# Late attention groups: reading all scores of a group first, sharing one weight buffer between three chunks, and turning the weights as a step of its own

## The chip, the core and the metric

The kernel runs on one NeuronCore of one Trainium2 chip. The metric is the device time of one execution in microseconds (us). A core has a matrix engine (PE, TensorE), whose weight loads are listed apart as PEld, a vector engine (DVE), a scalar engine (ACT), a general engine (POOL, GpSimd) and a sync engine (SP) that issues most DMA transfers. Every engine works off its own queue in order: an instruction that waits holds up all that stand behind it on the same engine.

## What is computed

Block-causal attention over 8 batches, 8 heads, 576 positions and head size 64, and a gated two-layer network on its output, all in float32:

```python
scores = q @ k.T / sqrt(64)                    # per batch and head
scores = where(block(i) >= block(j), scores, -1e9)   # blocks of 64 positions
attn = softmax(scores) @ v
x = attn, heads side by side                   # 4608 tokens x 512
h = x @ w_in                                   # 512 -> 2048
out = (h * sigmoid(1.702 * h)) @ w_out         # 2048 -> 512
```

## The kernel before

**Network.** The 4608 tokens are cut into 12 tiles of 384. For each of 16 slices `fc` of the hidden layer, `moe()` multiplies the tile with `w_in` (12 matmuls into a PSUM bank `hp`), ACT takes the tanh (line 621), DVE forms the gate (622), ACT rounds it to `gh` (633) and POOL takes the rest `gl` (through the helper `subtract`, line 83). The second product of a slice (9 matmuls into the banks `acc`) is issued only after the first product of the *next* slice, so that the gate has the time of one first product. Each product is made of three matmuls of high and low parts. At the end of a tile `split(t + 1)` cuts the next tile into `xh` (ACT, 557) and `xl` (DVE, 83).

**Attention.** Work goes by groups of one batch and two heads, 32 in all. The 576 query rows are five chunks (0 to 4) that see 64, 192, 320, 448 and 576 keys. `score` multiplies q and k into PSUM banks, chunks 3 and 0 side by side in one bank for each head, and 2 and 1 in another. `weigh` reads a score on DVE with the mask and a running extremum (line 378) into an SBUF tile `e`, and ACT takes the exponential in place, with its sum (385). `normalise` forms the reciprocal of the sum (DVE 395, 400) and scales `e`: on POOL (405), and for chunk 4 of a late group on DVE (407).

**Early and late groups.** Groups 0 to 7 are early: PE transposes their weights (`flip`). From group 8 on they are late: `turn` transposes 32 by 32 blocks on DVE (414, 419) into `turned`, and after chunk 4 it has SP issue 16 DMAs (426) that put these blocks in their places. `av` multiplies them with v. All late groups use the same two halves of `turned`: the turns of a group must wait for the 16 DMAs of the group before, which read what the turns write. A late group takes chunks 3, 0, 2 and 1 in `score`, and chunk 4 in `av` of the group before, in the step's item `V`. In `settle`, the loop of one bank pair is: read its chunks, then normalise and turn them, then go on to the next pair. The weight tile of chunk `i` is

```python
e = d2.tile([P, 2, w], F32, tag=f"e{i % 2}", name="e", bufs=1)
```

so that chunks 0, 2 and 4 take turns in one buffer, and chunks 3 and 1 in another: chunk 1 can't be read before chunk 3 is turned, nor chunk 2 before chunk 0 is.

**Score banks.** In the late stage `bank()` goes round three PSUM banks, `w0` to `w2`; a fourth is lent by the network, which otherwise alternates between two banks for `hp`. The outputs of `av` take banks from the same round, so `av` waits until the scores in them are read.

**The order of the work.** The PE order is written out by hand. `ORDER` gives each step (one group) a line of slots, 13 in a late step: an item, or `-` for nothing. After each slot `advance` issues network work up to a quota that grows evenly, and goes on to the next gate. `START` and `HANDOVER` are the lines of steps 4 and 8. On the other engines, the framework orders instructions by when they can start in its own estimate and by priority, not strictly as written; tanh, gate, `gh`, `gl` and `split` have a higher priority (`high_priority`). PE's matmuls and chunk 4's first `normalise` instruction keep the written order. One further order is forced: the third gate after a group's `score` is put behind the last score read on DVE (`behind`, 108 and 625 to 627).

Of the kernel before, what the change touches and what calls it, by code (L numbers as in the profile page):

```python
# [10 lines left out]
F32 = mybir.dt.float32  # L11
# [14 lines left out]
ORDER = (  # L26
# [3 lines left out]
)  # L30

START = "1+0 - B 2/3 L C - V - 4 - a - - -"
HANDOVER = "B C - 3+0/2+1 - - - - - - V - - - - -"


WEIGHTS_BY = ((0, 0), (8, 13), (14.5, 32))
# [4 lines left out]
def attention_moe_kernel(  # L41
# [9 lines left out]
    nc = tc.nc  # L51
    B, H, S, D = q.shape
    DM, DF = w_in.shape
    P = 128
    BLK = 64
# [7 lines left out]
    NPAIR = B * H // 2  # L63
    HP = H // 2
# [4 lines left out]
    d2 = ctx.enter_context(tc.tile_pool(name="d2", bufs=2))  # L69
# [5 lines left out]
    def early(n):  # L75

        return n < 2 * HP

    def phase(n):
        return 0 if n < HP else 1 if n < 2 * HP else 2  # L80
# [3 lines left out]

    turns = {"n": 0, "bank": 0, "experts": False, "late": False, "gates": 0}
    gate_bank = {"now": "h", "spare": "w3", "lent": False}
    conv = {"step": 0, "loaded": 0}

# [11 lines left out]
    def next_hp():  # L102
# [1 line left out]
            gate_bank["now"], gate_bank["spare"] = gate_bank["spare"], gate_bank["now"]  # L104
        gate_bank["lent"] = False
        return ps.tile([P, 512], F32, tag=gate_bank["now"], name="hp")

    def behind(ins, other):
        tc.add_manual_dep(
            ins.ins, other.ins.name, mybir.DependencyInfo(mybir.DependencyClass.NoSync, mybir.DependencyReason.DATA),  # L110
            reason="order on one engine",
        )

    def mm(**kw):
        return tc.keep_in_program_order(nc.tensor.matmul(**kw))  # L115
# [60 lines left out]
    es = []  # L176
# [4 lines left out]
    def width(i):  # L181
        return BLK * (2 * i + 1)
# [125 lines left out]
    def prep(n):  # L308

        tag = "e0" if early(n) and n % 2 else "qk"  # L310
        qk[n] = d2.tile([P, 2, S], F32, tag=tag, name="qk", bufs=1)
        for x in range(2):
            nc.vector.transpose(out=qk[n][:, x], in_=raw[n][:, x].rearrange("p c d -> p (c d)"))  # L313
        raw.pop(n)
        m = follower(n)
        if m is not None:
            load(m)
# [3 lines left out]
    def score(n, banks):  # L321

        turns["late"] = not early(n)
        turns["gates"] = 0
        if n not in stats:
            mx = d2.tile([P, NCH + 1, 2], F32, tag="mx", name="mx")
            sm = d2.tile([P, NCH, 2], F32, tag="sm", name="sm")
            stats[n] = (mx, sm)
        todo = []
        taken = 0  # L330
        for chunks in banks:

            part = []
            for lo, hi in ((0, 512),) if width(chunks[0]) <= 512 else ((0, 256), (256, S)):
                ss = []
                for _ in range(2):
                    taken += 1
                    ss.append(lent_bank() if taken == 1 and turns["late"] else bank())
                c = 0
                for i in chunks:  # L340
                    a, z = qrange(i)
                    w = min(hi, width(i)) - lo
                    for hd in range(2):
                        r = slice(hd * D, hd * D + D)

                        mm(
                            out=ss[hd][:, c : c + w], lhsT=qk[n][r, 0, a : a + P],
                            rhs=qk[n][r, 1, lo : lo + w], start=True, stop=True,
                        )
                        part.append((i, hd, lo, lo + w, ss[hd][0 : z - a, c : c + w]))  # L350
                    c += w
            todo.append(sorted(part, key=lambda x: (chunks[::-1].index(x[0]), x[2])))
        settle(n, banks, todo)

    def settle(n, banks, todo):
        for chunks, part in zip(banks, todo):
            e = {}
            for i, hd, lo, hi, s in part:
                e[i] = weigh(n, i, hd, lo, hi, s, e.get(i))
            if not early(n) and 4 in chunks and n + 1 < NPAIR:  # L360
                prep(n + 1)
            for i in chunks[::-1]:
                normalise(n, i, e[i])
                if not early(n):
                    turn(n, i, e[i])

    def weigh(n, i, hd, lo, hi, s, e):
        mx, sm = stats[n]
        a, z = qrange(i)
        m = z - a  # L370
        w = width(i)
        if early(n):
            e = es[i]
        elif e is None:
            e = d2.tile([P, 2, w], F32, tag=f"e{i % 2}", name="e", bufs=1)
        last = i > 0 and hi == w
        mk = mask[0:m, MW - (hi - lo) : MW] if last else mask[0:m, 0 : hi - lo]
        turns["read"] = nc.vector.tensor_tensor_reduce(  # L378
            out=e[0:m, hd, lo:hi], in0=s, in1=mk,
            op0=ALU.add, op1=ALU.min, scale=-0.125,  # L380
            scalar=3e38 if lo == 0 else mx[0:m, NCH, hd : hd + 1],
            accum_out=mx[0:m, i, hd : hd + 1] if hi == w else mx[0:m, NCH, hd : hd + 1],
        )
        if hi == w:
            nc.scalar.activation(  # L385
                out=e[0:m, hd], in_=e[0:m, hd], func=AF.Exp, scale=-1.0,
                bias=mx[0:m, i, hd : hd + 1], accum_out=sm[0:m, i, hd : hd + 1],
            )
        return e

    def normalise(n, i, e):
        _, sm = stats[n]
# [125 lines left out]
        return None if m is None or m >= NPAIR else m  # L518

    def order(n):  # L520
        return {HP: START, 2 * HP: HANDOVER}.get(n, ORDER[phase(n)]).split()

    def step(n):

        turns["n"] = n
        now = n < NPAIR

        def item(x):
            if x == "V":
                return (lambda: av(n - 1)) if n else None  # L530
            if x == "L":
                return (lambda: prep(n + 1)) if n + 1 < NPAIR else None
            if x in ("a", "B", "C"):
                m, chunks = {"a": (n, [0, 1]), "B": (n - 1, [2, 3]), "C": (n - 1, [4])}[x]
                return (lambda: flip(m, chunks)) if m >= 0 else None
            return (lambda: score(n, [[int(z) for z in y.split("+")] for y in x.split("/")])) if now and x != "-" else None

        return [item(x) for x in order(n)]
# [29 lines left out]
    def moe():  # L568
# [24 lines left out]
        for t in range(NT):  # L593
            tt = TILES[t][1]
            if t == 0:
                yield ("tile", 0)
                split(0)
            xh, xl = xs["xh"], xs["xl"]
            acc = [ps.tile([P, DM], F32, tag=f"acc{c}", name=f"acc{c}") for c in range(tt // P)]
            for fc in range(NFC):  # L600
                if t == 0:
                    convert(fc // FG * GROUP + NDC + fc % FG + 1)
                hp = next_hp()
                fs = slice(fc % FG * P, (fc % FG + 1) * P)
                terms = [(wa, xb, dc) for dc in range(NDC) for wa, xb in (("wih", xh), ("wil", xh), ("wih", xl))]
                if fc == 0:

                    terms.sort(key=lambda x: x[1] is xl)
                for cnt, (wa, xb, dc) in enumerate(terms):
                    mm(  # L610
                        out=hp[:, 0:tt], lhsT=weights(wa, fc // FG)[:, dc, fs], rhs=xb[:, dc, 0:tt],
                        start=cnt == 0, stop=cnt == 3 * NDC - 1,
                    )
                    if cnt % 3 == 2:
                        yield unit1(tt)
                g = d2.tile([P, TT], F32, tag="g", name="g", bufs=1)[:, 0:tt]
                gh = d2.tile([P, TT], F32R, tag="gh", name="gh")[:, 0:tt]
                gl = d2.tile([P, TT], F32R, tag="gl", name="gl")[:, 0:tt]

                with tc.high_priority(offset=300):  # L620
                    nc.scalar.activation(out=g, in_=hp[:, 0:tt], func=AF.Tanh, scale=1.702)  # L621
                    gate = nc.vector.scalar_tensor_tensor(  # L622
                        out=g, in0=g, scalar=1.0, in1=hp[:, 0:tt], op0=ALU.add, op1=ALU.mult
                    )
                    turns["gates"] += 1
                    if turns["late"] and turns["gates"] == 3:
                        behind(gate, turns["read"])

                if fc == NFC - 1 and t + 1 < NT:
                    yield ("tile", t + 1)  # L630
                    split(t + 1)
                with tc.high_priority(offset=300):
                    nc.scalar.copy(out=gh, in_=g)  # L633
                    subtract(nc.gpsimd, gl, g, f(gh))
                yield ("gate", fc)
                if prev is not None:
                    yield from second(prev)
                prev = (gh, gl, fc, acc, t)
# [88 lines left out]
```

## Time and profile before

| what | value |
| --- | --- |
| median of 3 runs | 1112.54 us (1110.59 to 1112.55) |
| the profiled execution | 1109.89 us |
| its span, first to last instruction | 1108.1 us |
| PE busy | 1065.1 us (96% of the span) |
| DVE, ACT, POOL busy | 585.0, 497.8, 405.1 us |
| late scores, first to last read on DVE | 187.0 to 938.8 us |

The profiled execution took 1.8 us more than its span and 2.65 us less than the median of the runs. In the profile, L378 is line 378 of the kernel; a releaser behind an arrow is what ended the idle time of an engine. Matmuls are pipelined and their ends are modelled, so PE's idle time is a lower bound of what PE loses. The program's tile names in the profile are `e` for the weights, `bank` for scores and attention outputs, `mx` and `sm` for extrema and sums, `g`, `gh`, `gl` for the gate and its parts. The turned weights and the DMAs between them are `turned`.

### The profile page before, as it was taken

The numbers are of one execution on the slowest core, as the hardware profiler recorded it, in microseconds if no ns is written. First come the engines' busy times: TensorE is split into PE (matmuls) and PEld (weight loads), VectorE is DVE, ScalarE is ACT, GpSimd is POOL, SyncE is SP. The second block draws the span as 40 slices with busy tenths as digits, with TensorE's granted clock in tenths as the row PEclk, the third lists the DMA queues.
The fourth block names the chain that finished last, engine by engine and source line by source line (L and its number), as shares of the span: only waits on it lengthen the run. The fifth ranks groups of instructions, "written<-read, shape, count | busy, mean of one in ns | idle before, by whom it ended". The sixth has DMA issues, their size and how long they took to land. (4 is left out here: it accounts for less than half of the span.)

```text
span 1108.1 us, 19988 instructions
## 1 busy us (share of the span) xinstructions
PE 1065.1 (96%) x6960; PEld 913.5 (82%) x6960; DVE 585.0 (53%) x1856; ACT 497.8 (45%) x1321; POOL 405.1 (37%) x509
## 2 busy tenths in 40 slices
PE   5969999989999999999999999999999999999998
PEld 3757777878888888788888888788888888999997
DVE  6786786555655655554555555455546655211211
ACT  6866776433533534444443543344444434332322
POOL 5665665323333233233333332333333333222222
PEclk9979999999999999999999999999999999999999
DMA  8634623432333443143444433244443322200000
GB/s 182 198 90 155 153 55 80 87 90 60 92 80 81 114 87 82 37 108 74 104 87 86 93 88 70 48 104 86 87 114 70 73 81 55 55 29 1 29 1 29
DMA packets 219365, 91.25 MB, mean 82 GB/s; under 512 B 197760, under 2 KB 197760, under 8 KB 219264
## 3 DMA queue, kind: packets, MB, share of 16 engines
q1 hardware_dynamic: 214528, 89.38, 34.2%
q8 instruction: 55, 0.90, 0.3%
q10 hardware_dynamic: 4736, 0.59, 0.3%
q14 instruction: 46, 0.38, 0.1%
HBM read 45.09 MB, written 9.44 MB: 49 GB/s over the span
## 5 line engine op out<-in xcount | busy, mean ns | idle before, releaser
L83 POOL TENSOR_TENSOR gl<-g,gh 128x384 fp32r<-128x384 f32 x192 | 194.1, 1011 | 501.0 <-ACT gh L633 345.4
L622 DVE SCALAR_TENSOR_TENSOR g<-g,hp 128x384 f32<-128x384 f32 x192 | 104.6, 545 | 323.7 <-ACT g L621 323.5
L115 PE MATMUL hp<-xh,wih 128*128 128x384 f32 x768 | 261.2, 340 | 4.0 <-DVE g L622 2.8
L621 ACT ACTIVATE g<-hp 128x384 f32<-128x384 f32 x192 | 94.4, 492 | 374.4 <-PE hp L115 319.7
L115 PE MATMUL hp<-xh,wil 128*128 128x384 f32 x768 | 258.5, 337 | 0.0
L115 PE MATMUL hp<-xl,wih 128*128 128x384 f32 x768 | 255.2, 339 | 0.7 <-DVE xl L83 0.5
L115 PE MATMUL acc<-woh,gh 128*128 128x512 f32 x576 | 233.0, 405 | 3.5 <-ACT gh L633 3.5
L115 PE MATMUL acc<-wol,gh 128*128 128x512 f32 x576 | 227.8, 396 | 0.0
L115 PE MATMUL acc<-woh,gl 128*128 128x512 f32 x576 | 168.1, 393 | 0.3 <-POOL gl L83 0.3
L405 POOL TENSOR_TENSOR e<-e,sm 64x64 f32<-64x64 f32 (+1 forms) x192 | 114.5, 612 | 135.3 <-ACT e L385 83.2
L115 PEld LDWEIGHTS hp<-xh,wih 128*128 128x128 f32 x768 | 144.4, 188 | 18.4 <-DVE g L622 4.6
L633 ACT CAST gh<-g 128x384 fp32r<-128x384 f32 x192 | 98.5, 513 | 124.5 <-DVE g L622 124.4
L115 PEld LDWEIGHTS hp<-xh,wil 128*128 128x128 f32 x768 | 144.4, 188 | 7.6
L115 PEld LDWEIGHTS hp<-xl,wih 128*128 128x128 f32 x768 | 143.9, 188 | 2.4 <-DVE xl L83 2.4
L385 ACT ACTIVATE e<-e,mx 64x64 f32<-64x64 f32 (+4 forms) x240 | 132.4, 555 | 26.0 <-DVE mx L378 26.0
L115 PEld LDWEIGHTS acc<-woh,gh 128*128 128x128 f32 x576 | 108.7, 189 | 32.1 <-ACT gh L633 8.3
L115 PE MATMUL bank<-qk 64*128 64x192 f32 (+5 forms) x768 | 120.0, 424 | 14.4 <-DVE qk L313 11.5
L115 PEld LDWEIGHTS acc<-woh,gl 128*128 128x128 f32 x576 | 108.0, 188 | 25.4 <-POOL gl L83 1.2
L115 PEld LDWEIGHTS acc<-wol,gh 128*128 128x128 f32 x576 | 109.0, 189 | 16.7 <-issue 0.4
L115 PEld LDWEIGHTS bank<-qk 64*128 64x128 f32 x768 | 68.8, 191 | 53.6 <-issue 15.9
L414 DVE STREAM_TRANSPOSE turned<-e 128x384 f32<-128x384 f32 (+1 forms) x192 | 89.8, 494 | 40.6 <-POOL e L405 33.2
L378 DVE CUSTOM_DVE_ANT_0 e<-bank,mask 64x64 f32<-64x64 f32 (+4 forms) x240 | 94.7, 444 | 25.5 <-PE bank L115 21.7
(50 smaller groups left out, 959.1 us busy)
## 6 DMA issues: line engine op xcount, KB each, us to landing
turned<-turned SPq DMA_DIRECT2D x192, 80.0 KB, 2.1
turned<-turned SPq DMA_DIRECT2D x96, 112.0 KB, 2.2
raw<-in_q_dram SPq DMA_DIRECT2D x128, 72.0 KB, 2.3
out_dram<-osb SPq DMA_DIRECT2D x36, 256.0 KB, 2.2
raw<-in_k_dram SPq DMA_DIRECT2D x120, 72.0 KB, 2.4
turned<-turned SPq DMA_DIRECT2D x96, 88.0 KB, 2.1
words<-in_moe_w_in_dram SPq DMA_DIRECT2D x16, 512.0 KB, 5.7
vp<-in_v_dram SPq DMA_DIRECT2D x60, 128.0 KB, 2.5
```

What stands on the lines that cost most here:

```text
L83: eng.tensor_tensor(out=out, in0=in0, in1=in1, op=ALU.subtract)
L115: return tc.keep_in_program_order(nc.tensor.matmul(**kw))
L378: turns["read"] = nc.vector.tensor_tensor_reduce(out=e[0:m, hd, lo:hi], in0=s, in1=mk, op0=ALU.add, op1=ALU.min, scale=-0.125, scalar=3e38 ...
L385: nc.scalar.activation(out=e[0:m, hd], in_=e[0:m, hd], func=AF.Exp, scale=-1.0, bias=mx[0:m, i, hd : hd + 1], accum_out=sm[0:m, i, hd : hd ...
L405: nc.gpsimd.tensor_tensor(out=x, in0=x, in1=sc.to_broadcast([m, width(i)]), op=ALU.mult)
L414: nc.vector.transpose(out=tw[:, :, SLOT[i] : SLOT[i] + i, hd].rearrange("p b j c -> p j b c"), in_=e[:, hd, 0 : i * P],)
L621: nc.scalar.activation(out=g, in_=hp[:, 0:tt], func=AF.Tanh, scale=1.702)
L622: gate = nc.vector.scalar_tensor_tensor(out=g, in0=g, scalar=1.0, in1=hp[:, 0:tt], op0=ALU.add, op1=ALU.mult)
L633: nc.scalar.copy(out=gh, in_=g)
```

## The change

For late groups, chunks 0 to 2 get one tile of 576 columns, side by side, from the buffer `e0`; chunk 3 has `e1` to itself, and chunk 4 takes `e0` as before. `settle` of the two bank pairs in `score` then only reads, and takes the exponentials; the chunks are kept in a list. A new item `T` normalises and turns all that is in the list. It stands three slots behind the scores in a late step. Step 8 has it four slots behind its scores, and step 9 gets a line of its own, with `T` in slot 6 and `V` in slot 9 instead of 7. Chunk 4 is read in `V` and then normalised and turned as before. The forced order of the third gate is taken out.

```diff
-    "3+0/2+1 - - - - - - V - - - - -",
+    "3+0/2+1 - - T - - - V - - - - -",
 )
-HANDOVER = "B C - 3+0/2+1 - - - - - - V - - - - -"
+HANDOVER = "B C - 3+0/2+1 - - - T - - V - - - - -"
+FIRST_LATE = "3+0/2+1 - - - - - T - - V - - -"
...
     def settle(n, banks, todo):
         for chunks, part in zip(banks, todo):
             e = {}
             for i, hd, lo, hi, s in part:
-                e[i] = weigh(n, i, hd, lo, hi, s, e.get(i))
-            if not early(n) and 4 in chunks and n + 1 < NPAIR:
-                prep(n + 1)
-            for i in chunks[::-1]:
-                normalise(n, i, e[i])
-                if not early(n):
-                    turn(n, i, e[i])
+                if i not in e:
+                    e[i] = es[i] if early(n) else weights_of(n, i)
+                weigh(n, i, hd, lo, hi, s, e[i])
+            if early(n):
+                for i in chunks[::-1]:
+                    normalise(n, i, e[i])
+            else:
+                weighed.extend((n, i, e[i]) for i in chunks[::-1])
+            if 4 in chunks and not early(n):
+                if n + 1 < NPAIR:
+                    prep(n + 1)
+                turn_all()
+
+    weighed = []
+    shared = {}
+
+    def weights_of(n, i):
+        if i > 2:
+            return d2.tile([P, 2, width(i)], F32, tag=f"e{i % 2}", name="e", bufs=1)
+        if n not in shared:
+            shared[n] = d2.tile([P, 2, S], F32, tag="e0", name="e", bufs=1)
+        return shared[n][:, :, BLK * i * i : BLK * (i + 1) * (i + 1)]
+
+    def turn_all():
+        for x in weighed:
+            normalise(*x)
+            turn(*x)
+        weighed.clear()
...
     def order(n):
-        return {HP: START, 2 * HP: HANDOVER}.get(n, ORDER[phase(n)]).split()
+        return {HP: START, 2 * HP: HANDOVER, 2 * HP + 1: FIRST_LATE}.get(n, ORDER[phase(n)]).split()
...
+            if x == "T":
+                return turn_all
...
-                    turns["gates"] += 1
-                    if turns["late"] and turns["gates"] == 3:
-                        behind(gate, turns["read"])
```

More of the change, by code (lines that the diff above doesn't have):

```diff
@@ L83, in subtract @@
         eng.tensor_tensor(out=out, in0=in0, in1=in1, op=ALU.subtract)
-    turns = {"n": 0, "bank": 0, "experts": False, "late": False, "gates": 0}
+    turns = {"n": 0, "bank": 0, "experts": False, "late": False}
     gate_bank = {"now": "h", "spare": "w3", "lent": False}
@@ L106, in next_hp @@
         return ps.tile([P, 512], F32, tag=gate_bank["now"], name="hp")
[L108 to L112, printed above, removed]
     def mm(**kw):
@@ L323, in score @@
         turns["late"] = not early(n)
-        turns["gates"] = 0
         if n not in stats:
@@ L371, in weigh @@
         w = width(i)
[L372 to L375, printed above, removed]
         last = i > 0 and hi == w
         mk = mask[0:m, MW - (hi - lo) : MW] if last else mask[0:m, 0 : hi - lo]
-        turns["read"] = nc.vector.tensor_tensor_reduce(
+        nc.vector.tensor_tensor_reduce(
             out=e[0:m, hd, lo:hi], in0=s, in1=mk,
@@ L388, in weigh @@
             )
-        return e
     def normalise(n, i, e):
@@ L621, in moe @@
                     nc.scalar.activation(out=g, in_=hp[:, 0:tt], func=AF.Tanh, scale=1.702)
-                    gate = nc.vector.scalar_tensor_tensor(
+                    nc.vector.scalar_tensor_tensor(
                         out=g, in0=g, scalar=1.0, in1=hp[:, 0:tt], op0=ALU.add, op1=ALU.mult
                     )
-                    turns["gates"] += 1
-                    if turns["late"] and turns["gates"] == 3:
-                        behind(gate, turns["read"])
                 if fc == NFC - 1 and t + 1 < NT:
```

## Prediction

> **What bounds the kernel now.** I read the page's busy times first, then busy time by stage, then who waited for whom on PE, and last the timelines around those waits.
>
> ```profile
> span 1108.1 us, 19988 instructions
> PE 1065.1 (96%) x6960; PEld 913.5 (82%) x6960; DVE 585.0 (53%) x1856; ACT 497.8 (45%) x1321; POOL 405.1 (37%) x509
> ```
>
> Busy time by stage (length, then PE, PEld, DVE, ACT, POOL, granted clock, DMA share), for the two stretches that hold the late groups:
>
> ```profile
> 185.00:243.00 58.00, 52.98 (x360) 44.65 (x359) 34.00 (x115) 25.16 (x70) 18.68 (x25) 0.97 0.30 68
> 243.00:940.00 697.00, 692.69 (x4600) 600.87 (x4600) 385.23 (x1276) 295.92 (x802) 236.44 (x308) 1.00 0.37 83
> ```
>
> PE sets the end. Of 697 us between 243 and 940 it idles 4.3, and 5.0 in the 58 us before. What is recoverable is what PE waits for between 185 and 945 (total, times, longest):
>
> ```profile
> PE bank L115 <- DVE mx L378: 3.9, 2, 1.9
> PE acc L115 <- ACT gh L633: 3.5, 1, 3.5
> PE hp L115 <- DVE g L622: 1.1, 1, 1.1
> PE hp L115 <- DVE xl L83: 0.5, 1, 0.5
> PE hp L115 <- ACT xh L557: 0.5, 2, 0.2
> ```
>
> That is 9.5 us in seven waits. The matmuls are the same before and after, and their order is by hand, so a wait that goes shortens the end by its length, and a wait that comes lengthens it. An untroubled group on DVE (start, duration):
>
> ```profile
> 403.86 0.21 DVE L378 CUSTOM_DVE_ANT_0 e<-bank,mask 64x64 f32<-64x64 f32 x1
> ...
> 406.44 0.17 DVE L395 TENSOR_SCALAR sm<-sm 128x2 f32<-128x2 f32 x1 [0.73 <-ACT e L385]
> ...
> 409.71 0.56 DVE L622 SCALAR_TENSOR_TENSOR g<-g,hp 128x384 f32<-128x384 f32 x1 [2.90 <-ACT g L621]
> 413.90 0.55 DVE L622 SCALAR_TENSOR_TENSOR g<-g,hp 128x384 f32<-128x384 f32 x1 [3.63 <-ACT g L621]
> 414.37 0.62 DVE L419 STREAM_TRANSPOSE turned<-e 64x128 f32<-64x128 f32 x2
> 415.03 1.04 DVE L414 STREAM_TRANSPOSE turned<-e 128x384 f32<-128x384 f32 x2
> 416.21 0.36 DVE L378 CUSTOM_DVE_ANT_0 e<-bank,mask 128x192 f32<-128x192 f32 x1
> ...
> 418.08 0.56 DVE L622 SCALAR_TENSOR_TENSOR g<-g,hp 128x384 f32<-128x384 f32 x1 [0.41 <-ACT g L621]
> ```
>
> Chunks 0 and 3 are read at 403.86, chunks 1 and 2 only at 416.21, behind the turns: two score banks stay taken for 12 us longer. Gates come every 4.19 us. How late may one be? The rounded gate and the matmul that uses it:
>
> ```profile
> 410.30 0.52 ACT L633 CAST gh<-g 128x384 fp32r<-128x384 f32 x1 [0.62 <-DVE g L622]
> ```
>
> ```profile
> 413.11 0.39 PE L115 MATMUL acc<-woh,gh 128*128 128x512 f32 x1
> ```
>
> `gh` of the 409.71 gate is done at 410.82 and needed at 413.11. So a gate may be 2.3 us late for nothing, and beyond that PE waits one for one.
>
> **Reads first.** The two waits on `mx` are in the steps where a tile ends inside the group:
>
> ```profile
> 452.07 1.62 DVE L83 TENSOR_TENSOR xl<-xr,xh 128x384 fp32r<-128x384 f32 x3 [5.81 <-ACT xh L557]
> ...
> 456.48 0.55 DVE L622 SCALAR_TENSOR_TENSOR g<-g,hp 128x384 f32<-128x384 f32 x1
> ```
>
> ```profile
> 456.21 2.10 PE L115 MATMUL bank<-turned,vp 128*64 128x128 f32 x40 [1.93 <-DVE mx L378]
> ```
>
> DVE stood 5.81 us before `xl`; the turns, the reads of chunks 1 and 2 and the forced gate were queued behind it, and `av` wanted a bank that those reads hold. After the change these reads have a buffer at once and stand some 12 us earlier, before any `xl`. The 3.9 us go. What is late next at that place is the gate; it no longer has to stand behind the reads. The four exponentials also move up, beside the tanh of the next gate:
>
> ```profile
> L385 ACT ACTIVATE e<-e,mx 128x320 f32<-128x320 f32 x44 | 24.2, 554 | 0.0
> ...
> L385 ACT ACTIVATE e<-e,mx 128x192 f32<-128x192 f32 x44 | 19.5, 448 | 4.8 <-DVE mx L378 4.8
> ```
>
> They are 2 x (0.554 + 0.448) = 2.0 us of ACT and end about when that tanh is due; a few tenths of delay lie under the 2.3 us. Reads take 1.5 us of DVE (416.21 to 417.67, where the idle time before the next gate begins) in an idle stretch of 2.9 us. Price: nothing on PE.
>
> **The first late step.** In step 8 a gate stands behind a turn that waits for POOL (1.1 us of PE, `hp` on `g`); with the reads first and the turns later, I count the 1.1 as gone. In step 9 the turns stand before their DMAs have ended:
>
> ```profile
> 217.04 0.31 DVE L419 STREAM_TRANSPOSE turned<-e 64x128 f32<-64x128 f32 x1 [1.21 <-DMA turned<-turned]
> 222.16 1.04 DVE L414 STREAM_TRANSPOSE turned<-e 128x384 f32<-128x384 f32 x2 [4.81 <-DMA turned<-turned]
> ...
> 224.72 0.55 DVE L622 SCALAR_TENSOR_TENSOR g<-g,hp 128x384 f32<-128x384 f32 x1
> ```
>
> ```profile
> 226.27 0.79 PE L115 MATMUL acc<-woh,gh 128*128 128x512 f32 x1 [3.45 <-ACT gh L633]
> ```
>
> The gate was due 4.2 us after the one at 215, near 219.3, and ran at 224.72, 5.4 late; less the 2.3 that makes 3.1, and PE idled 3.45. The clock of this stretch is 0.97: 0.03 x 58 = 1.7 us of full speed lost, and the matmul at 226.27 took 0.79 instead of 0.39. A part of that fell on the idle PE, so I take 1.5, between 1.0 and 2.0. The transfers that DVE waited for, and those of other steps, on SP:
>
> ```profile
> 208.99 11.56 SPq L426 DMA_DIRECT2D turned<-turned  x16
> ```
>
> ```profile
> 401.16 11.13 SPq L426 DMA_DIRECT2D turned<-turned  x16
> ```
>
> ```profile
> 432.75 10.29 SPq L426 DMA_DIRECT2D turned<-turned  x16
> ```
>
> Step length is 432.75 - 401.16 = 31.6 us, 2.4 a slot. `T` in slot 6 of step 9 is some 14.6 us behind the scores, past the third gate; the 16 issues end 10 us after the scores and have landed at 222, 12 us after them. So the turns are written behind the gate that they held up, and 3.5 + 1.5 = 5.0 us go. `V` two slots later costs no matmul, but puts chunk 4 and its 16 DMAs one network slice (4.2 us) later. In the untroubled group these DMAs land about 10.5 us after the first read (414.37 - 403.86, where the turn met no wait), so in step 10 they land near 14.7, while `T` there stands at 10 (three slots are 7.3 us, and then on to the next gate). DVE then waits 4.2 us, the third gate is up to 4 us late, and its matmul comes after `V`:
>
> ```profile
> 421.58 2.98 PE L115 MATMUL bank<-turned,vp 128*64 128x128 f32 x60
> 424.50 1.24 PE L115 MATMUL bank<-qk 64*128 64x384 f32 x8
> ```
>
> `V` gives that gate 4.1 us more room than the 2.3, so I count nothing here; without that cover it is 4 - 2.3 = 1.7 us, once. SP's own queue keeps its order: `prep`, loads and turned DMAs follow chunk 4 as before.
>
> **T in every group.** Its transposes on DVE:
>
> ```profile
> L419 DVE STREAM_TRANSPOSE turned<-e 64x128 f32<-64x128 f32 x110 | 33.6, 306 | 2.0
> ...
> L414 DVE STREAM_TRANSPOSE turned<-e 128x384 f32<-128x384 f32 x44 | 22.8, 557 | 2.2 <-DMA turned<-turned 1.2 <-issue 0.6
> ...
> L414 DVE STREAM_TRANSPOSE turned<-e 128x256 f32<-128x256 f32 x44 | 19.6, 446 | 29.7 <-POOL e L405 29.6
> ...
> L414 DVE STREAM_TRANSPOSE turned<-e 128x128 f32<-128x128 f32 x44 | 11.0, 283 | 0.2
> ```
>
> 4 x 0.306 + 2 x (0.557 + 0.446 + 0.283) = 3.8 us for chunks 0 to 3, as many as before but now together. Between two gates lie 4.19 - 0.55 = 3.6 us. Before, turns of 0 and 3 with the reads of 1 and 2 filled the same gap (414.37 to 418.08) without a wait of PE. The new block is 0.2 longer than the gap, and gates have priority: nothing, with an upper bound of 3.8 + 1.2 - 2.3 = 2.7 us a group if all of it, and a 1.2 us wait for POOL (29.7 us over 22 groups is 1.3), stood before one gate. Nothing less than zero is possible: untroubled groups have no PE wait to give. The shared buffer costs nothing: the turns end near 419.5, chunk 4's reads into it come after 424.5.
>
> A second load on DVE stands in these two rows:
>
> ```profile
> 420.05 0.44 DVE L395 TENSOR_SCALAR sm<-sm 128x2 f32<-128x2 f32 x1 [0.72 <-ACT e L385]
> ```
>
> ```profile
> 419.50 0.97 POOL L405 TENSOR_TENSOR e<-e,sm 128x192 f32<-128x192 f32 x2 [3.40 <-ACT e L385]
> ```
>
> An operation of 0.17 us (406.44) took 0.44 and ended with POOL's scaling at 420.47. The Trainium skill, "SBUF — State Buffer", section "Who interferes with whom", has it that a DVE `tensor_scalar` in a two-port mode and a GpSimd operation exclude each other for a whole instruction; by that rule every sum in `T` could stand behind a scaling, and the change would be slower. Reckoned from rows, three such operations a group can each lose at most one scaling of the 192 columns, 0.49 us, or about twice that for 448: 1.5 to 2.8 us. Alone that stays near the 2.3 us; it counts only on top of the block (slower rival).
>
> **The sum** against the profiled execution: 3.9 + 3.5 + 1.5 + 1.1 = 10.0 us off 1109.9, which is 1099.9. That execution was 2.65 us under the median, so 1102.5 as a median. The waits on `xl` and `xh` (1.0) may go too; I leave them.
>
> **The rivals.** (1) *T holds nothing back.* On DVE the order isn't the written one: at 406.44 chunk 3's normalise ran before chunk 0's turn at 414.37, which is written ahead of it. If the turns of step 9 are again put where their estimate, not their slot, has them, DVE waits for the DMAs as before and the 5.0 us stay: 1109.9 - 5.0 + 2.65 = 1107.5. Against it: chunk 4 of step 8 should be turned earlier. (2) *The wait moves to step 10.* The late DMAs of step 9 hold a gate that `V` does not cover; of 5.0 some 1.7 to 4 come back: 1104 to 1106.5. (3) *Slower: the block stands before a gate in every group.* 3.8 us of transposes, with 1.2 of POOL waits or the 1.5 to 2.8 of excluded sums, are 1.5 to 2.7 us beyond the slack. In 24 groups that is 36 to 65 us: 1138 to 1167. It decides once a group loses 10.0 / 24 = 0.42 us, that is when gates are more than 2.7 us late. For it: nothing forces a gate ahead any more. Against: 20 of 24 groups had this DVE work in that gap (413.90 to 418.08, all but 0.41 us full) and none of the seven waits. (4) *Nothing measurable*: single new waits eat the ten.
>
> **How the numbers follow.** Forecast (10.0 us, 1102.5) 0.50, with its own range 1099 to 1105.5; rival 1 0.18; rival 2 0.12; rival 3 0.14; rival 4 0.06. A measurement of this kernel can tell about 0.2% (2.2 us) from no change. Faster by more: 0.50 + nearly all of rivals 1 and 2 = 0.76. Within: 0.10. Slower: 0.14, rival 3. The range goes from 1098 (all 9.5 + 1.5 us gone, and runs as low as 1110.6 before) to 1112, which leaves out rival 3 and little else.
>
> **What would show it.** Right: reads of all four chunks within 4 us of the scores; no PE wait on `mx` after 243; no PE wait on `gh` near 222 and a clock of 1.00 there; DVE time of all groups unchanged. Wrong: waits of `acc` on `gh` in many steps (rival 3), one near 220 (1) or 250 (2), or a new releaser of `bank`.

## The result and the profile after

The changed kernel takes **1098.15 us** (median of 4 runs, 1097.56 to 1099.45); the kernel before takes 1111.72 (median of 4, 1110.59 to 1112.55). The ratio is 0.988, with a 95% interval of 0.9863 to 0.9897. The profiled execution took 1097.56 us, its span is 12.3 us shorter than before. The medians differ by 13.6, because the profiled execution of before, at 1109.89 us, lies below all four runs.

The page of the kernel after:

```profile
span 1095.8 us, 19944 instructions
PE 1063.1 (97%) x6960; PEld 913.4 (83%) x6960; DVE 603.6 (55%) x1856; ACT 499.3 (46%) x1321; POOL 403.9 (37%) x509
```

DVE does the same 1856 instructions, but is busy 18.6 us longer; the sums of 128x2 elements beside POOL's scalings, which are taken up below, alone take 70.5 us in the whole run where they took 32.2. The busy time by stage (length, then PE, PEld, DVE, ACT, POOL, granted clock, DMA share, GB/s):

```profile
185.00:243.00 58.00, 57.59 (x397) 48.80 (x396) 37.36 (x127) 28.04 (x79) 20.60 (x27) 1.00 0.33 74
243.00:930.00 687.00, 686.79 (x4575) 598.02 (x4574) 402.61 (x1271) 295.07 (x795) 233.29 (x306) 1.00 0.37 84
```

PE idles 0.4 us in the first stretch, where it idled 5.0, and 0.2 in the second, where it idled 4.3. The clock of the first stretch is 1.00 instead of 0.97. What PE waits for between 185 and 940 (total, times, longest):

```profile
PE hp L110 <- DVE g L634: 0.4, 1, 0.4
PE acc L110 <- POOL gl L84: 0.2, 1, 0.2
```

Seven waits with 9.5 us have become two with 0.6. An untroubled group on DVE, to be set against the one at 403.86 of before (L389 reads a score, L405 sums, L634 is the gate, L424 and L429 turn):

```profile
397.82 0.22 DVE L389 CUSTOM_DVE_ANT_0 e<-bank,mask 64x64 f32<-64x64 f32 x1
...
400.17 0.48 DVE L389 CUSTOM_DVE_ANT_0 e<-bank,mask 128x320 f32<-128x320 f32 x1
...
401.28 2.14 DVE L405 TENSOR_SCALAR sm<-sm 128x2 f32<-128x2 f32 x1 [0.27 <-ACT e L396]
...
403.81 0.53 DVE L634 SCALAR_TENSOR_TENSOR g<-g,hp 128x384 f32<-128x384 f32 x1
...
412.05 0.56 DVE L634 SCALAR_TENSOR_TENSOR g<-g,hp 128x384 f32<-128x384 f32 x1 [3.63 <-ACT g L633]
412.52 1.01 DVE L429 STREAM_TRANSPOSE turned<-e 64x128 f32<-64x128 f32 x4
416.23 0.56 DVE L634 SCALAR_TENSOR_TENSOR g<-g,hp 128x384 f32<-128x384 f32 x1 [2.70 <-ACT g L633]
416.70 2.07 DVE L424 STREAM_TRANSPOSE turned<-e 128x384 f32<-128x384 f32 x6
```

All chunks are read within 3 us of the first (before, 12 to 14 us). Then the first gate follows; the turns stand behind the third gate, and a second part of them behind the fourth. Every gate of this group still waits for its tanh, except the one at 403.81, which came right behind the sums. The ten turns take 1.01 + 2.07 = 3.1 us.

The third gate of step 9, where PE had idled 3.45 us:

```profile
218.11 0.56 DVE L634 SCALAR_TENSOR_TENSOR g<-g,hp 128x384 f32<-128x384 f32 x1 [3.29 <-ACT g L633]
222.02 0.55 DVE L634 SCALAR_TENSOR_TENSOR g<-g,hp 128x384 f32<-128x384 f32 x1 [3.36 <-ACT g L633]
222.49 0.64 DVE L429 STREAM_TRANSPOSE turned<-e 64x128 f32<-64x128 f32 x2
```

The gate waits for its tanh alone; the turns come behind it and no longer wait for a DMA.

**Where the 12.3 us went.** Matmul records show when a step starts, so the distance from one group's scores to the next gives what a step lost, idle or not. The first late scores start at 185.76 before and at 185.74 after. From there, the starts of the scores of steps 9, 10 and 11 on PE, before:

```profile
207.99 2.11 PE L115 MATMUL bank<-qk 64*128 64x448 f32 x16
244.67 2.11 PE L115 MATMUL bank<-qk 64*128 64x448 f32 x16
276.26 2.11 PE L115 MATMUL bank<-qk 64*128 64x448 f32 x16
```

and after:

```profile
206.57 2.11 PE L110 MATMUL bank<-qk 64*128 64x448 f32 x16
238.16 2.11 PE L110 MATMUL bank<-qk 64*128 64x448 f32 x16
270.22 2.11 PE L110 MATMUL bank<-qk 64*128 64x448 f32 x16
```

Step 8 is 1.4 us shorter, step 9 is 36.7 against 31.6, so 5.1, and step 10 is 32.1 against 31.6, so 0.5 longer. The first group in which a tile ends, before:

```profile
434.23 2.11 PE L115 MATMUL bank<-qk 64*128 64x448 f32 x16
468.97 2.11 PE L115 MATMUL bank<-qk 64*128 64x448 f32 x16
```

and after:

```profile
428.19 2.11 PE L110 MATMUL bank<-qk 64*128 64x448 f32 x16
459.78 2.11 PE L110 MATMUL bank<-qk 64*128 64x448 f32 x16
```

34.7 has become 31.6, the length of an untroubled step. The second such group does the same (690.12 to 724.84 before, 680.94 to 712.53 after): 3.15 + 3.13 = 6.3 us. The sum is 1.4 + 5.1 - 0.5 + 6.3 = 12.3, the whole difference of the spans.

### The profile page after: what moved, and what is told of

Read it like the earlier page. It is cut to its first block, busy times and chain, and to the rows that moved or that the text cites. A ratio compares the mean times of both kernels' runs of the same rounds, so it can differ in the third digit from the quotient of the medians.

```text
span 1095.8 us, 19944 instructions
## 1 busy us (share of the span) xinstructions
PE 1063.1 (97%) x6960; PEld 913.4 (83%) x6960; DVE 603.6 (55%) x1856; ACT 499.3 (46%) x1321; POOL 403.9 (37%) x509
## 4 chain that ended last, share of the span: by engine, by line
PE 89%; DVE 4%; ACT 2%; issue 2%; DMA 1%; SPq 1%; POOL 1%; POOLq 0%; DVEq 0%; ACTq 0%
PE hp L110 36%; PE acc L110 35%; PE bank L110 17%; PE bank L113 1%; ACT turned L396 1%; DMA raw<-in_k_dram 1%; SPq L290 1%; DVE wm L245 1%; DVE sm L405 1%; DVE qk L308 0%; DVE turned L389 0%; DVE e L389 0%; DMA words<-in_moe_w_out_dram 0%; DVE wm L240 0%; ACT e L396 0%
## 5 line engine op out<-in xcount | busy, mean ns | idle before, releaser
L634 DVE SCALAR_TENSOR_TENSOR g<-g,hp 128x384 f32<-128x384 f32 x192 | 104.9, 546 | 379.6 <-ACT g L633 379.5
L415 POOL TENSOR_TENSOR e<-e,sm 64x64 f32<-64x64 f32 (+1 forms) x192 | 111.7, 611 | 51.7 <-DVE sm L410 40.7
L389 DVE CUSTOM_DVE_ANT_0 e<-bank,mask 64x64 f32<-64x64 f32 (+4 forms) x240 | 92.8, 440 | 16.4 <-PE bank L110 15.2
L110 PEld LDWEIGHTS bank<-turned,vp 128*64 128x64 f32 x1800 | 85.4, 137 | 9.6 <-issue 6.6
```

Source lines behind the costliest of these rows:

```text
L389: nc.vector.tensor_tensor_reduce(out=e[0:m, hd, lo:hi], in0=s, in1=mk, op0=ALU.add, op1=ALU.min, scale=-0.125, scalar=3e38 if lo == 0 else ...
L415: nc.gpsimd.tensor_tensor(out=x, in0=x, in1=sc.to_broadcast([m, width(i)]), op=ALU.mult)
L634: nc.vector.scalar_tensor_tensor(out=g, in0=g, scalar=1.0, in1=hp[:, 0:tt], op0=ALU.add, op1=ALU.mult)
```

## The experiments

After the comparison two accounts stood against each other. The *buffer account*: the shared buffer lets all scores be read at once, and that carries all of the gain; the item `T`, its slot, the removed forced order and the new line of step 9 do nothing of their own. The *slot account*, that of the prediction: the reads carry the tile ends, and the slots of `T` and `V` carry the 5 us of step 9. Two further questions were the load of the sums on DVE, and how late a gate may be.

Each kernel was timed against the kernel before on the same chip. That took 1109.99 us beside the first four kernels (17 runs, 1108.73 to 1112.14) and 1110.91 beside the last four (13 runs, 1109.44 to 1113.00).

**Reads first, nothing else.** The kernel before with the shared buffer; `settle` reads both bank pairs and then turns at once. No `T`, no new line, and the forced order of the third gate stays. The main lines of the edit:

```diff
-                e[i] = weigh(n, i, hd, lo, hi, s, e.get(i))
+                if i not in e:
+                    e[i] = es[i] if early(n) else weights_of(n, i)
+                weigh(n, i, hd, lo, hi, s, e[i])
...
+        if not early(n):
+            turn_all()
```

> The kernel before with the shared buffer and the reads first; chunks 0 to 3 are turned right behind the reads, no T, no line of its own for step 9, and the third gate still forced behind the last read. Theory A (the reads first are nearly all of the gain, and they also take the turns of step 9 out of the gate's way, because the forced gate no longer has to wait for turns): about 1098 us, all of the 13 us, step 10's wait of 0.4 us gone, PE waits on mx gone in the groups that end a tile. Theory B (T and the line of step 9 take the 5 us there): the wait near 222 stays, about 1103 us.

1099.37 us (ratio 0.9896, 0.9883 to 0.9909), span 1094.9. The intervals of this kernel and of the full change overlap. The waits of PE from 185 to 940:

```profile
PE hp L115 <- DVE g L639: 0.4, 1, 0.4
```

and step 9 on DVE:

```profile
221.55 0.55 DVE L639 SCALAR_TENSOR_TENSOR g<-g,hp 128x384 f32<-128x384 f32 x1 [3.39 <-ACT g L638]
222.02 0.63 DVE L436 STREAM_TRANSPOSE turned<-e 64x128 f32<-64x128 f32 x2
```

The turns stand behind the third gate although no slot puts them there. The 5 us of step 9 go without `T` and without the new line: its scores and those of step 10 start 31.6 us apart (206.10 and 237.70). The groups in which a tile ends take 31.6 us too (427.26 to 458.85, 680.00 to 711.60), and the 0.2 us wait of step 10 isn't there.

**The buffer alone.** The kernel before, where only the weight tile changes; read, normalise and turn are written pair by pair as before, and the forced order stays. `weights_of` is that of the change.

```diff
-            e = d2.tile([P, 2, w], F32, tag=f"e{i % 2}", name="e", bufs=1)
+            e = weights_of(n, i)
```

> The kernel before with nothing but the shared buffer for chunks 0 to 2: the loop still says read a pair, normalise and turn it, read the next pair; the gate is still forced; no T, no new line. Theory A, since instructions of DVE, ACT and POOL are put where they can start and not as written: the reads of chunks 1 and 2 move ahead all the same, about 1098 us. Theory B': the written order (all reads, then all turns) matters: the reads stay behind the turns, about 1106 to 1111 us.

1097.78 us (0.9888, 0.9875 to 0.99), span 1096.6. The one wait of PE:

```profile
PE hp L115 <- DVE g L631: 1.5, 1, 1.5
```

This settles it for the buffer account: the change of the weight tile alone carries nearly all of the gain. Step 9 (207.87 to 239.47) and both groups in which a tile ends (429.03 to 460.62, 681.77 to 713.37) take 31.6 us. Even the written order of the reads is not needed: on DVE chunks 1 and 2 are read at 400.25 to 401.8, straight behind chunks 0 and 3 (398.65), since their buffer is free. What is left is the wait of step 8, 1.1 us before and 1.5 here, which goes to 0.4 where the reads are also written first. So the written order is worth about 1 us, and the new line costs 0.5 in step 10. In the medians neither can be told.

**The forced order alone.** The kernel before without the three lines that put the third gate behind the last read; its buffers as they were.

```diff
-                    turns["gates"] += 1
-                    if turns["late"] and turns["gates"] == 3:
-                        behind(gate, turns["read"])
```

> The kernel before without the forced order of the third gate, nothing else. Theory A: with the old buffers the reads of chunks 1 and 2 then fall behind the third and fourth gate, up to the beginning of V, and V waits some 3 us for its second bank in every one of 22 groups: 1111 + 60 = about 1170 us, with PE waits of bank on mx. The wait near 222 goes, since no gate is held by turns. Theory C (the forced gate itself was what cost the tile-ending groups and step 9, the buffer is incidental): faster, about 1100 us.

1176.0 us (1.0595, 1.0577 to 1.0613), span 1174.9: this part alone costs 66 us. The largest wait of PE, from 185 to 1020 because the late stage lasts longer here, and a group on DVE and on PE:

```profile
PE bank L115 <- DVE mx L378: 51.8, 22, 2.8
```

```profile
438.93 0.56 DVE L622 SCALAR_TENSOR_TENSOR g<-g,hp 128x384 f32<-128x384 f32 x1 [3.08 <-ACT g L621]
439.40 1.03 DVE L414 STREAM_TRANSPOSE turned<-e 128x384 f32<-128x384 f32 x2
440.57 0.36 DVE L378 CUSTOM_DVE_ANT_0 e<-bank,mask 128x192 f32<-128x192 f32 x1
```

```profile
441.68 2.10 PE L115 MATMUL bank<-turned,vp 128*64 128x128 f32 x40 [2.34 <-DVE mx L378]
```

Without the forced order the reads of chunks 1 and 2 stand behind the gate, not ahead of it, and `av` finds its banks taken in 22 groups. The stretch from 243 to 1000 has a granted clock of 0.98 here, 15 us of full speed in 757, which goes with the stalls. Not every stall costs clock: behind the one at 441.68 the clock is 1.00, but behind an equal one it is 0.50 from 406 to 409, and the same 40 matmuls take longer:

```profile
406.12 3.51 PE L115 MATMUL bank<-turned,vp 128*64 128x128 f32 x40 [2.34 <-DVE mx L378]
```

In step 9, however, the wait of `acc` on `gh` is gone: the gates run at 219.24 and 223.43, the turns come behind them from 223.90 on, and none of them waits for a DMA.

**The line of step 9 alone.** The kernel before with `V` in slot 9 of step 9; there is no `T` in it.

```diff
+FIRST_LATE = "3+0/2+1 - - - - - - - - V - - -"
...
-        return {HP: START, 2 * HP: HANDOVER}.get(n, ORDER[phase(n)]).split()
+        return {HP: START, 2 * HP: HANDOVER, 2 * HP + 1: FIRST_LATE}.get(n, ORDER[phase(n)]).split()
```

> The kernel before with V in slot 9 instead of 7 in step 9, nothing else. Theory A: the turns of step 9 still stand before the gate and wait for the DMAs, so the wait near 222 stays: 1111.7 within 1.5 us. Theory B (the line of step 9 takes the 5 us): about 1106.5 us.

1110.88 us (12 runs, 1.0004, 0.9993 to 1.0015). The waits:

```profile
PE bank L116 <- DVE mx L379: 3.9, 2, 1.9
PE acc L116 <- ACT gh L634: 2.9, 1, 2.9
```

Near 222 the wait is 2.9 instead of 3.5 us, and nothing is won that can be measured.

**`T` in another slot.** The kernel after, with `T` in the first slot behind the scores instead of the third, in steps 10 to 31.

```diff
-    "3+0/2+1 - - T - - - V - - - - -",
+    "3+0/2+1 T - - - - - V - - - - -",
```

> The changed kernel with T directly behind the scores (slot 1 instead of 3) in steps 10 to 31. Theory A (where T is written says nothing to DVE, ACT and POOL): the same time, 1098 within 1 us, and the turns at the same distance from the scores, some 16 us. Theory B (T's slot holds the turns back): the turns begin some 4 us earlier, before the DMAs of the group before have landed, and the time changes by several us.

1097.98 us (0.988, 0.9865 to 0.9895), the time of the kernel after, and the same two waits of PE. In a normal group the first read is at 398.37, and:

```profile
412.60 0.55 DVE L634 SCALAR_TENSOR_TENSOR g<-g,hp 128x384 f32<-128x384 f32 x1 [3.63 <-ACT g L633]
413.07 1.01 DVE L429 STREAM_TRANSPOSE turned<-e 64x128 f32<-64x128 f32 x4
```

The turns start 14.7 us behind the first read, as in the kernel after (412.52 - 397.82), behind the same gate. The slot of `T` moves nothing.

**Scaling on ACT.** The kernel after, with the weights of chunks 0 to 3 scaled on ACT instead of POOL.

```diff
-SCALE_ON = ("PPPPP", "PPPPP", "PPPPD")
+SCALE_ON = ("PPPPP", "PPPPP", "AAAAD")
```

> The changed kernel with the scaling of chunks 0 to 3 of late groups on ACT instead of POOL. If the sums on DVE that take over 2 us each group are held by POOL's scalings (both want the same SBUF access), their longest drops from 2.3 us to about 0.25 and DVE's busy time between 243 and 930 falls by 22 x 2 = 44 us or so, from 402.6 to about 359. If they are long for another reason (waiting for ACT's sums, counted as busy), they stay long. In both cases PE hardly notices, since DVE has room: 1098 within 2 us; ACT gets about 4 us more work a group.

1100.08 us (0.9892, 0.9876 to 0.9909): not to be told from the kernel after. The sums on DVE between 243 and 930 in the kernel after, and here:

```profile
L405 DVE TENSOR_SCALAR sm<-sm 128x2 f32<-128x2 f32 x88 | 57.7, 656 | 20.6 <-ACT e L396 20.5
```

```profile
L405 DVE TENSOR_SCALAR sm<-sm 128x2 f32<-128x2 f32 x87 | 14.4, 166 | 36.5 <-ACT e L396 36.4
```

DVE's whole busy time there falls from 402.6 to 361.3 us, by 41 us, and the time does not. In the kernel after, the slow sum is the one at 401.28: it ends at 403.42, and POOL's four scalings beside it are

```profile
401.07 2.32 POOL L415 TENSOR_TENSOR e<-e,sm 64x64 f32<-64x64 f32 x4 [1.59 <-DVE sm L410]
403.77 2.33 POOL L415 TENSOR_TENSOR e<-e,sm 128x192 f32<-128x192 f32 x4 [0.37 <-DVE sm L405]
```

The first four end at 403.39, 0.03 us ahead of the end of the sum. Beside the next four the gate at 403.81 takes its usual 0.53. The rule of the Trainium skill that the prediction weighed ("SBUF — State Buffer", "Who interferes with whom") agrees in that the `tensor_scalar` is held and the gate, which reads one operand from SBUF and one from PSUM, is not. It speaks of one whole instruction, and the kernel with the buffer alone fits that:

```profile
402.11 0.90 DVE L404 TENSOR_SCALAR sm<-sm 128x2 f32<-128x2 f32 x1 [0.20 <-ACT e L394]
...
403.20 0.70 DVE L404 TENSOR_SCALAR sm<-sm 128x2 f32<-128x2 f32 x1
```

```profile
402.05 4.11 POOL L414 TENSOR_TENSOR e<-e,sm 128x448 f32<-128x448 f32 x6 [0.70 <-DVE sm L409]
```

Its two sums end at 403.01 and 403.90, with the first and the second of six scalings back to back (0.93 us each for 128x448), not with the run. In the kernel after, the first of these sums stood until the whole run of four was over. That POOL's scalings hold the sums is shown by moving them to ACT; what decides how many of them a sum must let by is not shown. The 2 us a group lie in the time in which DVE waits for the tanh, so PE does not see them, but for a part in step 10.

**Gates made late.** The kernel after with three, and with six, more instructions of the gate's shape ahead of each gate in the last two tiles (32 slices, no attention beside them); their results are not used.

```diff
+                    for _ in range(3 if t >= 10 else 0):
+                        more = d2.tile([P, TT], F32, tag="e0", name="more", bufs=1)[:, 0:tt]
+                        nc.vector.scalar_tensor_tensor(
+                            out=more, in0=g, scalar=1.0, in1=hp[:, 0:tt], op0=ALU.add, op1=ALU.mult
+                        )
```

> The changed kernel with three more DVE operations of the gate's size (3 x 0.545 = 1.6 us) before every gate of the last two tiles, 32 slices, their results unused. The prediction's slack of 2.3 us says: no change, 1098 within 1.5 us. If a gate has no slack, 32 x 1.6 = 52 us more.

> As the run before with six such operations, 3.3 us, before every gate of the last two tiles. The slack of 2.3 us says: about 1.0 us for each of some 31 slices, 1098 + 31 = 1129 us, with PE waits of acc on gh. If the slack were 4.2 us (a whole first product), no change.

With three 1113.49 us (1.0025, 1.0014 to 1.0036), with six 1170.09 (1.0529, 1.0513 to 1.0544): 15 and 72 us over the kernel after, 0.5 and 2.2 us a slice. With six, PE waits for `gh` in all 32 slices. So 2.3 us are not free where every slice is late. Between tanh and `gh` there are 1.1 us in the kernel after (1041.61 and 1042.73), 2.9 with three and 4.7 with six (1039.87 and 1044.58). ACT and POOL with three:

```profile
1040.79 0.49 ACT L633 ACTIVATE g<-hp 128x384 f32<-128x384 f32 x1 [1.13 <-POOL gl L84]
1043.74 0.51 ACT L647 CAST gh<-g 128x384 fp32r<-128x384 f32 x1 [2.45 <-DVE g L639]
1045.37 0.49 ACT L633 ACTIVATE g<-hp 128x384 f32<-128x384 f32 x1 [1.12 <-POOL gl L84]
```

```profile
1044.33 1.01 POOL L84 TENSOR_TENSOR gl<-g,gh 128x384 fp32r<-128x384 f32 x1 [3.57 <-ACT gh L647]
```

There is one tile `g`. The next tanh writes it, and must wait until POOL has taken `gl` from it, which ends at 1045.34, 0.03 us before the tanh at 1045.37. Tanh, gate, `gh` and `gl` form a loop; with three it takes 4.58 us, 0.39 over the 4.19 of PE, and with six 6.35 (1039.87 to 1046.22). Of the added 1.8 and 3.6 us this leaves 1.4 us a slice free, where the lateness repeats; what is beyond it is lost one for one.

## Why the prediction was right, point by point

**Direction and size.** Forecast 1102.5, measured 1098.15: faster, as the likeliest case had it, but 4.35 us beyond its point, 0.85 beyond its own range of 1099 to 1105.5, and just inside the whole range. That it lies inside is partly luck: the lower end of 1098 is not what its own figures give (1110.6 less 9.5 and 1.5 is 1099.6). Of the 4.35, the sum was 2.3 too small (10.0 against 12.3): the tile ends came 2.4 us, step 8 0.3 and step 9 0.1 above their terms, and step 10 took back 0.5. The other 2.05 are the step from the profiled execution to the median: 2.65 was added, and after it is 0.6 (1097.56 to 1098.15).

**The step that was mis-sized: the tile ends.** Predicted 3.9 us, the idle time of two waits on `mx`; measured 6.3. The mechanism was right. The prediction left out 0.5 us of waits on `xh`, which lie in the same two groups and went too. The other 1.9 was not listed as idle time. Most of it lies in the slice at the tile end, whose 12 matmuls are spread over 2.95 us before,

```profile
461.75 0.45 PE L115 MATMUL hp<-xh,wih 128*128 128x384 f32 x1
...
463.31 0.44 PE L115 MATMUL hp<-xh,wih 128*128 128x384 f32 x1 [0.24 <-ACT xh L557]
...
464.70 0.39 PE L115 MATMUL acc<-woh,gh 128*128 128x512 f32 x1
```

where the same slice takes 2.1 after (453.40 to 455.50). Only 0.24 of these 0.85 us is listed as a wait, and in the second group it is much the same (717.64 to 720.59). "A wait that goes shortens the end by its length" gave a lower bound; the start-to-start distance is the measure.

**Step 9: the right amount by a wrong reason.** Predicted 3.5 + 1.5 = 5.0, measured 5.1, and the clock there is 1.00. But the step "`T` in slot 6 of step 9 is ... past the third gate ... So the turns are written behind the gate" fell: rival 1 was right that `T` holds nothing back (`T` two slots earlier in all later steps moves no turn; without any `T` the turns stand behind the gate too), and yet the 5 us did not stay. What held the gate was a chain in the old code: the third gate was forced behind the last read, that read waited for the buffers, these for the turns, and these for the 16 DMAs. On an in-order engine the turns had to stand ahead of that gate. The chain breaks at either end: by the forced order (its removal ends the wait of step 9 too, though it loses 66 us elsewhere) or by the buffers. With the old buffers either order loses against the kernel after: some 12 us with the reads ahead of the gate, some 78 with the reads behind it. The new line leaves the chain whole, and the wait at 2.9. That the order on DVE follows an estimate and not the written slots was quoted in the prediction for rival 1, and then not carried through: the question was not where the slot stands but what the estimate may not reorder.

**Step 8: near by luck.** Predicted 1.1, measured 1.4, but made up otherwise. The wait of `hp` on `g` fell from 1.06 to 0.41 us, so 0.65 of the 1.1 went. The other 0.75 is a stall on `xl`, which the prediction had left out and which isn't there after:

```profile
203.45 0.44 PE L115 MATMUL hp<-xl,wih 128*128 128x384 f32 x1 [0.51 <-DVE xl L83]
```

**`V` two slots later.** Predicted nothing in step 10; it lost 0.5. This is rival 2 in small, by another releaser than foreseen. The late chunk 4 kept DVE until 240.66, so the reads of step 10 began 2.6 us behind the start of its scores (238.16 to 240.80), where the group at 397.82 has 1.2. Sums, gate and the eight scalings came later too; the gate ran at 247.09, 1.3 us after its tanh, and PE waits for `gl` on POOL:

```profile
247.05 2.33 POOL L415 TENSOR_TENSOR e<-e,sm 128x192 f32<-128x192 f32 x4 [0.37 <-DVE sm L405]
249.34 1.01 POOL L84 TENSOR_TENSOR gl<-g,gh 128x384 fp32r<-128x384 f32 x1
```

`gl` stands behind four scalings that end at 249.38, and its matmul at 250.41 starts 0.2 us late. The reads-first kernel without the line has no such wait (step 10: 31.6). With the scalings on ACT step 10 is as long (32.1), and PE waits for `gh` instead, so the loss does not hang on POOL alone.

**The turns in every group.** Predicted nothing, with a slower rival at 1138 to 1167. Right: the ten turns take 3.1 us back to back, where 3.8 was added up from single ones, and lie in two gaps with a gate between them. "For it: nothing forces a gate ahead any more" did not matter. The excluded sums, 1.5 to 2.8 us a group by the estimate, came at 2.0 ((57.7 - 14.4) / 22 groups). That the size fits is luck: three sums were to lose one scaling each, and one sum lost all of it. They stand ahead of a gate whose tanh ends at 403.64, which is less than 0.2 us late for them. By these sums one of the signs named for being right failed: the DVE time did not stay unchanged (+18.6 us).

**The slack.** "A gate may be 2.3 us late for nothing, and beyond that PE waits one for one" is near for one gate (before, 5.4 late gave 3.45 idle, so 2.0 were free). Where every gate is late it is 1.4 us, because the loop through `g` binds first. Rival 3's price stayed unpaid not because the room is large but because hardly a gate is late.

What stays open is by which numbers the framework's estimate places the turns behind the third gate: the runs show that it does so for every slot tried, not why.

## What to carry to other kernels

Where instructions on one engine form a chain through buffers and forced orders, look for the chain, not for the slot: here three chunks side by side, in a buffer that was there and wide enough, were worth nearly the whole gain, and the forced order that had been worth 66 us became needless. Size a stall by the distance of the same matmul from step to step, since a stretched sequence of matmuls is only partly listed as a wait. And the room that one late instruction has is not the room of a lateness in every round; look for the single buffer that closes the loop.

## What the runs showed of the hardware

A sum of 128x2 elements on DVE, 0.17 us alone, took 2.1 to 2.3 us beside POOL in every late group of the kernel after but the first: it stood until a run of four scalings issued back to back was over. With the buffer alone two such sums took 0.9 and 0.7 us, each until one scaling of a run of six was over. With the scalings on ACT the mean of the sums fell from 656 to 166 ns. The reciprocals of the same size, which with the buffer alone run beside the scalings too, stayed at a mean of 162 ns.

The granted clock was 0.98 over 757 us with 21 stalls of some 2.3 us, in the kernel without the forced order, and 1.00 over 687 us of the kernel after, which has one of 0.2. Of two equal stalls of 2.34 us one left it at 1.00, and behind the other it was 0.50 for some 3 us.
